# A token's own term in a chunked RWKV attention: from products by tokens in place of score columns with u

## The chip, the cores and the metric

The kernel runs on one core of a Trainium2 chip. The core's engines, which run side by side and meet at semaphores, are TensorE (PE, with its weight loads PEld), VectorE (DVE), ScalarE (ACT), GpSimd (POOL) and SyncE (SP, which here only starts DMAs). The metric is the device time in microseconds; lower is better. All numbers are float32.

## The reference, cut to what matters

The first half is an RWKV-5 recurrence over 768 tokens, for 4 batches and 8 heads of width 48; the second is a router that sends each of the 3072 tokens to one of 8 experts.

```python
for t in range(S):                                   # S = 768, B = 4, H = 8, D = 48
    kt, vt, rt = (k[:, :, t], v[:, :, t], r[:, :, t])
    cur = np.einsum('bhd,bhe->bhde', u[None] * kt, vt)
    y[:, :, t] = np.einsum('bhd,bhde->bhe', rt, state + cur)
    state = w[None, :, :, None] * state + np.einsum('bhd,bhe->bhde', kt, vt)
x = y.transpose(0, 2, 1, 3).reshape(B * S, H * D)    # 3072 x 384
# router: the expert with the largest cosine to x, gate = its softmax weight
# out[rows of e] = gate * (relu(x @ w1[e]) @ w2[e])
```

The term with `u` joins a token with itself alone: it adds `(sum over d of u[d] * k[t,d] * r[t,d]) * v[t]` to `y[t]`. That sum is one number for a token and a head. It is the part of the work that the change treats.

## The kernel before, in words

**Chunks and turns.** The 768 tokens are cut into 6 chunks of 128. A turn is one chunk for two of the four batches (`u` = 0 or 1 inside the turn, not to be confused with the input `u`), so there are 12 turns, 0 to 11. Turns of even number bring the first two batches of a chunk, odd ones the other two. In a chunk the decay is taken apart into a power of `w` that scales K and one that scales R (`kpow`, `rpow`, tables that are built once), so that the product of a scaled K and a scaled R carries the decay between the two tokens. A chunk is worked in two halves `s` of 64 tokens, and heads in pairs `p` with a parity `par`.

**One turn.** For turn t the work is: load K, R, V (SP); scale R and K by tokens on POOL (`scale_r` L376-379, `scale_k` L371-373: 128x384 each, two of each in a turn); turn them so that the width stands on the partitions (`turn_in` L390-393, transposes on PE into the PSUM banks `D`); take them out of PSUM (`take_in` L396-410, ACT copies, 128x512 each, into `RT` and `KT`); the scores (`scores` L425-440, PE); mask them to what lies before the token (`mask` L447-451, VectorE, four of 128x256); the outer products for the state (`outer` L460-472, PE), which VectorE adds (`half_state`, `next_state` L479-490) and POOL decays (`decay_state` L493-496); and a turn later the values times the scores (`with_v` L515-528), the state times R (`with_state` L531-545), the turning back (`turn_y` L554-558), and what the router needs (`take_x`, `keep_x`, `squares`, then in every second turn the logits and the choice of an expert in small VectorE steps).

**The own term.** `RT` holds two kinds of R side by side, index `j`: plain, and times `u*w`. The second is made by `own_r` (L413-422): a VectorE product of 128x512 that reads PSUM, two in a turn (in turn 0 eight ACT scalings instead). A score matmul therefore has 128 moving columns, 64 of each kind (L433-436), and writes both into one bank. `own_terms` (L454-458) then puts the diagonal of the second kind into the masked scores `AT`: four predicated copies of 128x256 in a turn, whose data lie in PSUM.

**Banks and order.** There are eight PSUM banks: four `D`, two `U`, two `Y`. `turn_in` writes the same `D` banks as the scores, so the transposes for turn t+1 wait until `mask` and `own_terms` of turn t have read them. The order on every engine is written out by hand: `plan.at(time, function)` gives each piece a place in a turn of `PERIOD = 9.4`, the pieces are sorted by that number and issued in that order. The numbers are places in a queue and not times; each engine then works through its queue as its waits allow. In a turn that begins with its scores at 0 and 0.9, the next turn's `turn_in` stand at 3.3, 3.77, 5.65 and 6.12, `with_v` at 1.8 and 4.25, `with_state` at 2.3, `outer` at 4.75 and `turn_y` of the turn before at 6.65 and 7.1. On POOL the next turn's scalings stand at 1.0, 2.0, 3.0 and 4.0 and the decay at 6.8; the first scaling also waits for the first scores of the running turn, by a dependency set by hand (L378-379).

**Around it.** Before the turns `build_first` (L82-132) loads `w` and `u` as columns in 4-byte pieces, builds the tables and the first loads; `tables_rows` turns them into `kpow` and `rpow`. After the turns come the experts, which keep PE busy until the outputs are scattered.

## Time and profile before

| | us |
|---|---|
| median of 3 runs | 421.48 |
| lowest and highest of them | 415.93, 426.96 |
| the profiled execution | 415.55 |
| its span | 413.7 |
| start of the scores of turn 0, of turn 11 | 8.81, 115.69 |
| TensorE clock granted, mean | 0.964 |

The start of a turn below is the start of its first score matmul in the timeline of PE: 8.81, 15.49, 24.25, 34.94, 44.41, 55.28, 64.70, 76.14, 85.28, 95.75, 105.70, 115.69 for turns 0 to 11. From turn 3 to turn 11 that is 80.75 us for four pairs of turns, 20.2 us a pair. Matmuls count as two records each in the trace, so that the 32 score matmuls of a turn are 64 records.

The rows of the groups of instructions that the change touches, cut from the view of groups with shapes kept apart; the columns are line, engine, operation, output <- inputs, shapes, count, then busy us and mean ns of one, then idle time before them:

```profile
L433 PE MATMUL ps<-RT,KT 48*64 48x128 f32 x768 | 25.3, 275 | 0.2
L448 DVE TENSOR_TENSOR AT<-ps,smask 128x256 f32<-128x256 f32 x48 | 18.6, 414 | 1.2 <-PE ps L433 1.2
L418 ACT ACTIVATE RT<-RT,uw 128x128 f32<-128x128 f32 x8 | 2.5, 390 | 0.0
```

### The profile page before, as it was taken

The page shows a single profiled execution, that of the slowest core. Times are in us where ns is not written, and L with a number is a line of the kernel's source. Part 1 is how long each engine was busy: PE and PEld are TensorE (multiplying, and loading weights), DVE is VectorE, ACT ScalarE, POOL GpSimd, SP SyncE. Part 2 cuts the span into 40 slices and gives each one's busy share as a digit, 9 for nine tenths or more (in the row PEclk, how much of TensorE's full clock was granted, in tenths as well). Part 3 has the DMA queues.
Part 4 walks back from the last instruction along what each step waited for, and adds up shares of the span by engine and source line. Part 5 has one row for each costly group of instructions (what it writes and reads, how often), then busy time and mean ns, then how long its engine had stood idle before and what let it go on. Part 6 is the DMA issues. An engine that isn't in the chain of part 4 may idle for free.

```text
span 413.7 us, 12753 instructions
## 1 busy us (share of the span) xinstructions
PE 383.0 (93%) x5055; PEld 349.9 (85%) x5055; DVE 236.4 (57%) x603; ACT 138.2 (33%) x357; POOL 189.2 (46%) x222
## 2 busy tenths in 40 slices
PE   8889899999989996999989997699999999999993
PEld 5778788888878895989779997699999989989982
DVE  7957787878885650532843744155546546465331
ACT  4464546465524521221023212221321321422410
POOL 3875656555530354420377427501753855702002
PEclk9999999999996996899999999689999999999998
DMA  9988788788154573263953553144454446101001
GB/s 157 198 165 174 158 172 181 146 183 179 44 178 142 162 238 104 73 164 93 315 178 90 126 182 93 42 111 136 132 137 142 144 133 199 62 10 57 0 2 65
DMA packets 100232, 54.44 MB, mean 132 GB/s; under 512 B 80897, under 2 KB 95275, under 8 KB 100162
## 3 DMA queue, kind: packets, MB, share of 16 engines
q1 hardware_dynamic: 93218, 43.68, 41.6%
q0 software_dynamic: 4448, 9.45, 7.5%
q8 instruction: 42, 0.69, 0.7%
q10 hardware_dynamic: 2496, 0.40, 0.5%
q14 instruction: 28, 0.23, 0.2%
HBM read 44.25 MB, written 9.58 MB: 130 GB/s over the span
## 4 chain that ended last, share of the span: by engine, by line
PE 76%; issue 9%; DVE 2%; another core or an unknown queue 2%; POOL 1%; ACT 1%; POOLq 0%; DVEq 0%; ACTq 0%
PE ps L1243 9%; PE ps L1383 8%; PE ps L1165 7%; PE ps L1364 6%; PE pu L1243 5%; PE ps L433 4%; PE ps L393 4%; PE pu L1383 4%; PE py L1243 4%; PE py L1383 3%; PE pu L558 3%; PE py L524 3%; PE py L1165 3%; PE py L543 2%; PE pu L469 2%
## 5 line engine op out<-in xcount | busy, mean ns | idle before, releaser
L1123 POOL DMA_INDIRECT G<-xs,quarters x76 | 83.7, 1101 | 50.5 <-issue 38.8
L1342 POOL DMA_INDIRECT out_dram<-y,goes x27 | 28.3, 1048 | 97.0 <-DVE y L1352 41.3
L1165 PE MATMUL ps<-RT,w 128*128 128x128 f32 x204 | 30.1, 299 | 4.4 <-ACT R L1168 1.9
L1165 PEld LDWEIGHTS ps<-RT,w 128*128 128x128 f32 x204 | 27.3, 210 | 5.9 <-issue 2.3
L377 POOL TENSOR_TENSOR Rw<-R,rpow 128x384 f32<-128x384 f32 x22 | 22.8, 1037 | 14.2 <-PE ps L433 8.0
L1243 PE MATMUL ps<-xTe,w 128*128 128x192 f32 (+3 forms) x132 | 27.0, 339 | 0.0
L433 PE MATMUL ps<-RT,KT 48*64 48x128 f32 x768 | 25.3, 275 | 0.2
L433 PEld LDWEIGHTS ps<-RT,KT 48*64 48x64 f32 x768 | 21.1, 132 | 3.7 <-issue 2.5
L373 POOL TENSOR_TENSOR Kw<-K,kpow 128x384 f32<-128x384 f32 x22 | 23.8, 1081 | 0.5 <-DMA R<-in_r_dram 0.5
L1243 PEld LDWEIGHTS ps<-xTe,w 128*128 128x128 f32 x132 | 23.4, 194 | 0.1
L496 POOL TENSOR_TENSOR T<-T,wC 128x384 f32<-128x384 f32 x10 | 8.3, 827 | 27.1 <-DVE T L490 27.1
L448 DVE TENSOR_TENSOR AT<-ps,smask 128x256 f32<-128x256 f32 x48 | 18.6, 414 | 1.2 <-PE ps L433 1.2
L409 ACT COPY RT<-ps 128x512 f32<-128x512 f32 x22 | 12.9, 585 | 18.3 <-PE ps L393 16.9
L455 DVE COPY_PREDICATED AT<-dmask,ps 128x256 f32<-128x256 int32 x48 | 18.5, 441 | 0.0
L1270 ACT ACTIVATE RT<-RT 128x384 f32<-128x384 f32 (+1 forms) x18 | 9.5, 532 | 26.1 <-DVE RT L1182 18.6
L1243 PE MATMUL ps<-Tx,S 128*128 128x192 f32 (+3 forms) x76 | 16.5, 348 | 1.2 <-issue 1.1
L420 DVE TENSOR_TENSOR RT<-ps,uw 128x512 f32<-128x512 f32 x22 | 15.2, 690 | 4.2 <-ACT RT L409 3.9
L393 PE MATMUL ps<-ident,Rw 128*128 128x128 f32 x96 | 15.4, 283 | 2.2 <-DVE AT L455 1.0
L1383 PE MATMUL ps<-T,RT 128*128 128x192 f32 x96 | 17.3, 327 | 0.0
L1270 ACT ACTIVATE hT<-hT 128x432 f32<-128x432 f32 (+2 forms) x18 | 9.7, 541 | 21.2 <-DVE hT L1182 16.1
L1383 PEld LDWEIGHTS ps<-T,RT 128*128 128x128 f32 x96 | 15.9, 190 | 0.9
L469 PE MATMUL pu<-V,Kw 64*64 64x48 f32 x704 | 14.4, 218 | 2.4 <-issue 2.3
(380 smaller groups left out, 917.0 us busy)
## 6 DMA issues: line engine op xcount, KB each, us to landing
w<-in_moe_w_dram SPq DMA_DIRECT2D x96, 128.0 KB
w<-in_moe_w_dram SPq DMA_DIRECT2D x24, 384.0 KB
xs<-X SPq DMA_DIRECT2D x24, 192.0 KB
K<-in_k_dram SPq DMA_DIRECT2D x32, 96.0 KB
R<-in_r_dram SPq DMA_DIRECT2D x32, 96.0 KB
V<-in_v_dram SPq DMA_DIRECT2D x32, 96.0 KB
w<-in_moe_w_dram SPq DMA_DIRECT2D x16, 192.0 KB
V<-in_v_dram SPq DMA_DIRECT2D x8, 192.0 KB
```

Source lines behind the costliest of these rows:

```text
L373: q.tensor_mul(of(k.Kw, t)[:, u, :, 0:D], of(k.K, t)[:, u] if t else raw(k, 0)[:, u, :, 0:D], k.kpow)
L377: ins = k.nc.gpsimd.tensor_mul(of(k.Rw, t)[:, u, :, 0:D], of(k.R, t)[:, u], k.rpow)
L393: k.last = k.nc.tensor.transpose(bank[:, p * C : (p + 1) * C], pair(src[:, u], p), k.ident)
L433: ins = k.nc.tensor.matmul(k.D[2 * u + par][halves(s), p * C : (p + 1) * C], KT[rows, u, p, halves(s)], RT[rows, u, p, s].rearrange("q j i ...
L469: k.last = k.nc.tensor.matmul(k.U[s][par * DP : (par + 1) * DP, col : col + D], Kw[halves(s), u, h, :], V[halves(s), u, h, 0:D], start=Tru ...
L1123: k.nc.gpsimd.indirect_dma_start(out=k.GG[e % 2][:, g * QUARTER : (g + 1) * QUARTER], out_offset=None, in_=k.xs.rearrange("n (q c) -> (n q ...
L1165: k.last = k.nc.tensor.matmul(ps, w1[:, m, f * 128 : (f + 1) * 128], x_of(k, e, m)[:, cols], start=(m == 0), stop=(m == NK - 1))
L1243: k.last = nc.tensor.matmul(ps[:, i * h : (i + 1) * h], a[:, g, i * 128 : (i + 1) * 128], b, start=start and i == 0, stop=True, skip_group ...
L1270: nc.scalar.activation(out(i, c), out(i, c), ACT.Relu)
L1342: k.nc.gpsimd.indirect_dma_start(out=out[:, :], out_offset=IndirectOffsetOnAxis(ap=k.goes[0:n, e, t : t + 1], axis=0), in_=y[0:n, :], in_o ...
L1364: k.last = k.nc.tensor.matmul(k.two[e][m], a, b, start=(f == 0), stop=(f == NF - 1))
L1383: k.last = nc.tensor.matmul(ps, a(q), b[:, q], start=start and q == 0, stop=True, skip_group_check=True,)
```

## The change

The own term no longer goes through the scores. Each token's K and R, as they lie by tokens, are multiplied (`product`: 128x384, on POOL, but for one of turn 0 on VectorE), then multiplied by `u` (turn 0, whose K and R are unscaled) or `u*w` (`with_u`, VectorE, in place), and summed over the 48 of a head (`own_sums`, VectorE, 128x384 to 128x8). `own_terms` now spreads these sums along the diagonal: one predicated copy of 128x512 for each `u`, with its data in SBUF, in place of two of 128x256 with their data in PSUM. `own_r` and the second kind in `RT` go; a score matmul has 64 moving columns. The room of the second kind holds the products `KR`. `u` comes as a row of 384 and is spread to all partitions by a matmul with a row of ones and an ACT copy (`spread_u`, twice); the row of `w` for it, loaded later before, is loaded at the start. `kp` is made by ACT as a reversed copy. The K scaling of turn 0 goes from VectorE to POOL.

The order of a turn changes: one `turn_y` of two moves behind the first scores of the next turn but one (with its `take_x`, `keep_x`, `squares`), the four `turn_in` are put between other pieces, `with_state` and `outer` are each cut in two, and `half_state` stands behind the second `outer`. `choose_a` of the chunk before the last moves from 1.0 to 2.3.

```diff
-        for dst, src in ((wc, k.w), (uw, k.u)):
-            for s in range(2):
-                q = nc.sync if s == 0 else nc.scalar
-                q.dma_start(out=dst[s * DP : s * DP + D, :], in_=src.rearrange("(p s) d -> s d p", s=2)[s])
+        for s in range(2):
+            q = nc.sync if s == 0 else nc.scalar
+            q.dma_start(out=wc[s * DP : s * DP + D, :], in_=k.w.rearrange("(p s) d -> s d p", s=2)[s])
+    k.w_row, k.u_row, k.uw_row = k.X[2][0:1, 1], k.X[2][0:1, 0], k.X[1][0:1, 1]
+    for q, dst, src in ((nc.sync, k.w_row, k.w), (nc.scalar, k.u_row, k.u)):
+        q.dma_start(out=dst, in_=src.rearrange("(o h) d -> o (h d)", o=1))
...
+    nc.gpsimd.tensor_scalar(k.uw_row, k.w_row, W_MIN, W_MAX, ALU.max, ALU.min)
+    nc.gpsimd.tensor_mul(k.uw_row, k.uw_row, k.u_row)
...
-    kp = scratch(k.YT[1], 1, NP)
-    nc.vector.tensor_mul(kp, t[:, :, ::-1], over_i)
     rp = scratch(k.YT[0], 0, NP)
     nc.vector.tensor_mul(rp, t, over_i)
-    k.uw = k.aconst.tile([128, NP], F32, name="uw2")
-    nc.vector.tensor_mul(k.uw, uw, wc)
+    kp = scratch(k.YT[1], 1, NP)
+    nc.scalar.copy(kp, rp[:, :, ::-1])
...
+def spread_u(k, i):
+    k.nc.tensor.matmul(k.Y[i][:, 0:DM], k.ones[0:1, :], (k.u_row, k.uw_row)[i], start=True, stop=True)
+    k.nc.scalar.copy(k.u_all[:, i], k.Y[i][:, 0:DM].rearrange("q (h d) -> q h d", h=H))
...
 def scale_k(k, t, u):
-    q = k.nc.gpsimd if t else k.nc.vector
-    q.tensor_mul(of(k.Kw, t)[:, u, :, 0:D], of(k.K, t)[:, u] if t else raw(k, 0)[:, u, :, 0:D], k.kpow)
+    k.nc.gpsimd.tensor_mul(of(k.Kw, t)[:, u, :, 0:D], of(k.K, t)[:, u] if t else raw(k, 0)[:, u, :, 0:D], k.kpow)
...
-def own_r(k, t, u):
-    if t == 0:
-        for p in range(NP):
-            R = of(k.RT, t)[:, u, p]
-            k.nc.scalar.mul(R[:, :, 1, :], R[:, :, 0, :], k.uw[:, p : p + 1])
-        return
-    k.nc.vector.tensor_mul(
-        of(k.RT, t)[:, u, :, :, 1, :], k.turned[u][0].rearrange("q (p s i) -> q p s i", p=NP, s=2),
-        k.uw[:, :, None, None].to_broadcast([128, NP, 2, HC]),
-    )
+def product(k, t, u):
+    a, b = (of(k.Kw, t), of(k.Rw, t)) if t else (raw(k, 0), raw(k, 1))
+    q = k.nc.vector if (t, u) == (0, 1) else k.nc.gpsimd
+    q.tensor_mul(of(k.KR, t)[:, u], a[:, u, :, 0:D], b[:, u, :, 0:D])
+def with_u(k, t, u):
+    q = k.nc.gpsimd if (t, u) == (0, 0) else k.nc.vector
+    KR = of(k.KR, t)[:, u]
+    q.tensor_mul(KR, KR, k.u_all[:, 1 if t else 0])
+def own_sums(k, t, u):
+    k.nc.vector.reduce_sum(of(k.own, t)[:, u], of(k.KR, t)[:, u], axis=AX.X)
...
-                    k.D[2 * u + par][halves(s), p * C : (p + 1) * C], KT[rows, u, p, halves(s)],
-                    RT[rows, u, p, s].rearrange("q j i -> q (j i)"),
+                    k.D[2 * u + par][halves(s), p * HC : (p + 1) * HC], KT[rows, u, p, halves(s)],
+                    RT[rows, u, p, s],
...
-def own_terms(k, t, u, par):
+def own_terms(k, t, u):
+    shape = [128, 2, NP, HC]
     k.nc.vector.copy_predicated(
-        of(k.AT, t)[:, u, par].rearrange("q (p i) -> q p i", p=NP),
-        k.dmask[:, None, :].to_broadcast([128, NP, HC]), kinds(k, u, par)[:, :, 1],
+        of(k.AT, t)[:, u].rearrange("q r (p i) -> q r p i", p=NP),
+        k.dmask[:, None, None, :].to_broadcast(shape),
+        of(k.own, t)[:, u].rearrange("q (p r) -> q r p", r=2)[:, :, :, None].to_broadcast(shape),
     )
...
-            plan.at(before + (4.0 if t else 4.75) + 2.6 * u, own_r, k, t, u)
+                if t:
+                    plan.at(before + ((2.75, 3.8), (5.3, 6.35))[u][place], turn_in, k, t, u, which)
+                    plan.at(before + ((3.4, 4.4), (6.1, 6.8))[u][place], take_in, k, t, u, which)
...
+            if t:
+                plan.at(before + 5.0 + u, product, k, t, u)
+                plan.at(before + 6.9 + 0.5 * u, with_u, k, t, u)
+                plan.at(before + 7.0 + 0.5 * u, own_sums, k, t, u)
+            else:
+                when = (before + 4.0, at + 2.3)[u]
+                for i, fn in enumerate((product, with_u, own_sums)):
+                    plan.at(at + 1.55 if (u, i) == (0, 2) else when + 0.01 * i, fn, k, t, u)
...
-                plan.at(at + 1.65 + 1.5 * u + 0.4 * par, own_terms, k, t, u, par)
+            plan.at(at + 1.65 + 1.5 * u, own_terms, k, t, u)
...
-            plan.at(at + 4.75, outer, k, t)
-            plan.at(at + 5.6, half_state, k, t)
+            for u in range(2):
+                plan.at(at + 4.75 + u, outer, k, t, (u,))
+            plan.at(at + 6.16, half_state, k, t)
...
-            plan.at(nxt + a[1], with_state, k, t)
+            for s in range(2):
+                plan.at(nxt + a[1] + s, with_state, k, t, (s,))
...
-                plan.at(nxt + a[5] + 0.45 * u, turn_y, k, t, u)
+                over = u * (P + 0.5 - a[5])
+                plan.at(nxt + a[5] + over, turn_y, k, t, u)
...
+    plan.at(-P + 3.2, spread_u, k, 0)
+    plan.at(1.0, spread_u, k, 1)
     for u in range(2):
-        plan.at(0.05 + 0.01 * u, scale_k, k, 0, u)
+        plan.at(0.05 + 2.0 * u, scale_k, k, 0, u)
```

## The prediction

> **What bounds the kernel now.** I read the page's busy shares first, then busy time in one stretch per turn, then the timeline of two turns.
>
> ```profile
> PE 383.0 (93%) x5055; PEld 349.9 (85%) x5055; DVE 236.4 (57%) x603; ACT 138.2 (33%) x357; POOL 189.2 (46%) x222
> ...
> 44.41:55.28 10.87, 9.79 (x317) 8.77 (x317) 7.32 (x21) 6.52 (x20) 6.57 (x9) 1.00 0.80 168
> 55.28:64.70 9.42, 9.42 (x293) 8.44 (x289) 8.07 (x22) 4.38 (x13) 5.14 (x5) 1.00 0.77 165
> 64.70:76.14 11.44, 10.05 (x317) 8.83 (x316) 8.08 (x27) 6.52 (x20) 6.93 (x10) 1.00 0.81 169
> 76.14:85.28 9.14, 9.14 (x297) 8.30 (x293) 8.08 (x22) 4.42 (x13) 5.19 (x5) 1.00 0.76 163
> ```
>
> The first line shows busy time by engine. The others give, per turn (4 to 7): length, then busy time of PE, PEld, VectorE, ACT and POOL with counts, the clock, the DMA share. In turns 5 and 7 TensorE is busy for the whole turn; in 4 and 6 it lacks 1.1 and 1.4 us, mostly "issue", in which nothing in the trace holds it. So in the turns TensorE is the bound, and its work is worth its own length. VectorE's busy 8 us leave about 2.
>
> ```profile
> 57.77 0.69 PE L524 MATMUL py<-AT,V 64*64 64x64 f32 x32
> 58.28 0.63 PE L543 MATMUL py<-RT,T 48*48 48x64 f32 x32
> 58.73 0.63 PE L543 MATMUL py<-RT,Tmid 48*48 48x64 f32 x32
> 61.72 1.10 PE L469 MATMUL pu<-V,Kw 64*64 64x48 f32 x64
> 64.70 2.28 PE L433 MATMUL ps<-RT,KT 48*64 48x128 f32 x64
> ```
>
> Timeline of PE: start, duration, what. The 64 score records of a turn take 1.9 to 2.3 us. The next lines stand 0.45 us apart for 32 records with 64 moving columns and the same 48 rows.
>
> ```profile
> 45.70 1.00 POOL L377 TENSOR_TENSOR Rw<-R,rpow 128x384 f32<-128x384 f32 x1
> 45.86 0.88 DVE L665 TENSOR_TENSOR l<-l,inv 128x32 f32<-128x32 f32 x1
> 56.52 1.24 POOL L377 TENSOR_TENSOR Rw<-R,rpow 128x384 f32<-128x384 f32 x1 [1.29 <-PE ps L433]
> 56.82 1.49 DVE L844 TENSOR_TENSOR P<-slot,lo 128x512 f32<-128x512 f32 x1
> 57.72 1.47 POOL L373 TENSOR_TENSOR Kw<-K,kpow 128x384 f32<-128x384 f32 x1
> ...
> L665 DVE TENSOR_TENSOR l<-l,inv x6: 191/880/882, 45.9 to 141.0; 128x32 f32<-128x32 f32 x6
> L844 DVE TENSOR_TENSOR P<-slot,lo x6: 684/1086/1494, 56.8 to 141.1; 128x512 f32<-128x512 f32 x6
> L373 DVE TENSOR_TENSOR Kw<-Kw,kpow x2: 546/904/1262, 9.5 to 10.7; 128x384 f32<-128x384 f32 x2
> ```
>
> This is the second view that matters (durations in the last three lines: least, median, most, in ns). A VectorE step whose two inputs both lie in SBUF takes 191 ns alone and 880 beside a POOL product; it ends as that product ends (45.86 + 0.88 = 46.74 against 46.70). `P` costs 684 alone and 1494 between two scalings, and the POOL product behind it 1.47 in place of 1.0. They take turns.
>
> **What the skill says.** The Trainium skill, SBUF — State Buffer, section "Who interferes with whom": a VectorE instruction with two SBUF inputs contends with a GpSimd one that reads SBUF; the second waits for the first to end; with one SBUF input it does not; a reduction never does. The trace agrees on the first: 880 against 191. It also agrees that masks, with one input in PSUM, are free: 407 to 425 ns beside any POOL work. VectorE: DVE Perf Modes, section "The TRN2 errata — SBUF-src ops pay a fixed extra latency per instruction", has (N+151)/0.96 ns for an fp32 two-input product: 557 for 384, 691 for 512. The trace has 546 and 684. TensorE: Matmul & The Clock Gate, "Part 3: Packing small matmuls — row/col tiling": matmuls in different parts of the array run together. The trace agrees: 64 records of 269 ns pass in 1.91.
>
> **The change part by part.**
>
> *TensorE.* Scores at 64 columns: 64 records x 0.45/32 = 0.90 for 1.91, so -1.0 us a turn, -12 over 12 turns; all of it is on the path while TensorE is the bound. `spread_u` adds 2 x 2 records at 384 columns; 12 such took 3.87 (chain, line 1364), so 0.65 each. The first stands ahead of turn 0's transposes and lies open: +0.65. The new order has the same matmuls; I cost it at nothing, since transposes and small matmuls never waited for each other in turns 5 and 7.
>
> *VectorE.* Gone in a turn: two `own_r`, 0.60 apart in the timeline, and four copies, 0.33 apart: 2.5. Added: two copies of 512, not in the trace. Lower bound 0.60 (as `own_r`, same size), upper 0.69 (formula): 0.60, plus 0.07 each since they follow the second mask at once: 1.34. Two `with_u` at 0.55 (row L373 alone), two sums. The nearest reduction, of 384, took 0.528; I take 0.53. A step that needs the one before stood 0.66 behind it (`half_state`, `next_state`), an independent one 0.46: 2 x (0.66 + 0.46) = 2.24. Net +1.1 a turn. Over a pair of turns VectorE's queue was full for 16.9 us (20.86 between turns 5 and 7, less 3.97 of listed idle), 1.2 of it waits for POOL. So 15.7 + 2.2 = 17.9 of own work, beside TensorE's 20.2 - 2.0 = 18.2.
>
> *POOL.* +2 products a turn of the kind of `scale_k` and `scale_r`, 1.0 each (0.965 from start to start): busy 5.9 to 7.9 a turn. In turn 0: product, `with_u` and two scalings, 4.0, ahead of or between the scalings for turn 1. Two one-row steps for `uw_row` not in the trace, between 0.2 (small memset) and 1.0 (product of the same 384): 0.6 each, hidden by waiting for K and R.
>
> *The shared port.* A ledger per pair of turns. POOL's reads: before 8 x 0.965 + 2 x 0.83 = 9.4, now 12 x 0.965 + 1.66 = 13.2. (The `pow` of `choose_a` is not counted: at 116.5 `P` took its 0.69 beside it.) VectorE's steps with two SBUF inputs: before `P` 0.60, `QV` 0.34 and nine small ones at 0.2, 2.7; now also 4 x 0.6 of `own_terms`, whose data move from PSUM to SBUF, and 4 x 0.5 of `with_u`: 7.1. Sum 12.1 before, 20.3 now, against 20.2 a pair today. That is the core of it. `own_terms` stands at 1.65 and 3.15, amid POOL's scalings at 1.0 to 4.0, `with_u` beside the second product and the decay. No trace shows a predicated copy waiting for POOL: the bounds are nothing (then 17.9 in the ledger) and one POOL product, 0.97, each. I take half a product. With eight new steps that is 3.9 if POOL is always at work; POOL reads 13.2 of 20.2, so 2.5. VectorE: 17.9 + 1.2 + 2.5 = 21.6 if none hides in present idle; about 0.7 hides in waits for PE that shorten, so 20.9. What queues behind a waiting `own_terms` is the next two masks; turn_in of the next turn waits for them, and then the scores. So I take 20.9 a pair, +0.7, over the five pairs of turns 1 to 10: +3.5.
>
> *Start.* ACT's eight scalings (8.36 to 10.90) no longer hold scores 0, and VectorE's masks no longer stand behind two K scalings (9.50 to 11.23): -1.5, bound -2.5. But POOL must do 9 products in turn 0, from 8.5 on, then four memsets of V (1.05) and two more products; its first scaling for turn 2 starts at about 19.5, not 16.73, and scores 2 follow it: +2.8. With 0.65 for `spread_u`, +2. DMA: 768 pieces of 4 bytes less 384, two rows of 1.5 KB moved ahead of K and R on SP's and ACT's queues (issue 0.26 each): nothing either way, within 0.5, since K and R are met first by matmuls that end at 6.07.
>
> *End.* Turn 11 has no scalings beside it: its scores keep their -1.0. `turn_y`, its squares and `choose_a` move by up to 1.3 places, still before `choose` at 4.2. ACT's moved steps (copies 0.48, squares 0.52) lie in its idle time: it is busy 4.4 to 7 of 10 us. Weight loads hang on PE's progress and move along. Experts: unchanged. -1.
>
> *Sum:* +3.5 + 2 - 1 = +4.5 on the profiled 415.55: 420. The median of the runs shown, 421.48, is 1.4% above that execution, so a median of **426**.
>
> **Rivals.** *A, the saving stays (faster).* The waits for POOL fall into time that VectorE would idle, or the copies don't hold the port. Then TensorE sets 18.2 + 0.3 a pair: -1.7 x 5.5 = -9.4, -1 at the end, +1 at the start: -9.5, median 412. For it: TensorE's bound is plain. Against it: the ledger, and VectorE's 17.9 leaves only 0.3 for waits. *B, POOL and the port become the chain (slower beyond 2%).* Each VectorE step with two inputs, the small ones of the router too, meets a POOL product and they alternate. In the 19 steps of a pair with half a product each at 80% that is 7.4 of waits, less the 2.5 + 1.2 counted: +3.7, of which half shifts into idle: 22.7 a pair, +2.5 x 5 = +12.5, with +2 - 1: +13.5, median 435. It decides from +1.5 a pair on, 21.7. For it: `P` and `l` already meet a product nearly each time (medians 1086 and 880). Against: POOL stops after its six products until the decay. *C, the scores don't get shorter,* since the weight loads (133 ns for 64 columns, 120 in lines 543) set their pace: 64 loads of 120 pass in 0.90, so 64 of 133 in about 1.0, and 0.9 is saved all the same; small, and inside the ranges of the others.
>
> **How the numbers follow.** The likeliest case, a near balance a little slower, 0.50: 420 to 432. A 0.22: 407 to 417. B 0.28: 429 to 445. The range 411 to 438 leaves about 0.1 below (the lower half of A) and 0.1 above (the upper third of B). Two percent, 8.4 us, is about what a measurement of this kernel can tell from no change: its three runs spread by 2.6%. Faster: the larger part of A and none else, 0.18. Slower: most of B and a tenth of the middle case, 0.31. Within: 0.51.
>
> **What would show it.** In the changed profile: 64 score records in about 0.9 to 1.1 us (else C). `own_terms` at 0.6 to 0.7 alone and up to 1.7 with POOL at work; if all 24 stay under 0.75, the copy doesn't hold the port, and A gains. `with_u` between 0.55 and 1.5. VectorE full in the turns and TensorE no longer: waits of PE's transposes for AT, KT or POOL's Kw of over 0.3 a turn. Pairs of turns at 20.9; 18.5 shows A, over 21.7 B. First scaling for turn 2 at 19 to 20. Wrong would be: turns of 9.2 with PE still full.

## The result, and the profile after

The changed kernel takes 456.86 us median (452.92 to 460.29, 5 runs); beside it the kernel before took 420.1 (412.85 to 426.96, 5 runs). The ratio is 1.095, with a 95% interval from 1.081 to 1.109: slower. The median lies above the predicted range (426, 411 to 438). (Executions of one kernel fall into a faster and a slower state, and a ratio with an interval is taken over the faster ones alone, so that it is not the quotient of the medians.) The profiled execution of the changed kernel has a span of 455.0 us, 41.3 more than the 413.7 of before. Line numbers below are those of the changed kernel (`scores` L448, `turn_in` L403, `mask` L459, `with_u` L434, `own_sums` L438, `own_terms` L468, `product` L428).

Busy time by engine, from the page, to set beside the line of before:

```profile
PE 398.9 (88%) x5059; PEld 355.9 (78%) x5059; DVE 264.3 (58%) x600; ACT 140.9 (31%) x352; POOL 228.3 (50%) x250
```

TensorE's share falls from 93% to 88%, although its records are as many as before but for four more (the two matmuls of `spread_u`), and those of the scores are narrower. Where the time lies is seen from the starts of the turns. Scores 0 start 1.2 us later than before (9.97), scores 2 5.2 later (29.47), scores 11 40.8 later (156.46). From scores 11 to the end it is 298.5 us, before 298.0. So 35.6 of the 41.3 us lie in turns 2 to 10, which go from 91.4 to 127.0 us. (One more profile of each kernel, on another chip, splits its 42.4 us into 4.8 up to scores 2, 32.5 in turns 2 to 10 and 5.2 after them.) Busy time in one stretch per turn, for turns 4 to 7 (columns as in the prediction: length, busy PE, PEld, VectorE, ACT, POOL, clock, DMA):

```profile
57.42:68.62 11.20, 9.83 (x318) 8.05 (x317) 9.98 (x25) 6.68 (x18) 10.73 (x12) 1.00 0.71 151
68.62:85.53 16.91, 13.16 (x294) 11.10 (x290) 10.45 (x25) 4.97 (x13) 7.26 (x9) 0.70 0.41 91
85.53:96.67 11.14, 9.97 (x317) 8.23 (x317) 9.92 (x25) 6.66 (x18) 10.71 (x12) 1.00 0.70 152
96.67:112.61 15.94, 12.26 (x293) 10.20 (x289) 10.33 (x25) 4.96 (x13) 6.55 (x7) 0.79 0.46 97
```

Even turns are little longer than the 10.87 and 11.44 of before; turns 5 and 7 take 16.91 and 15.94 where they took 9.42 and 9.14. VectorE is busy 10.45 and 9.92 us in turns 5 and 6, 20.4 for the pair, about what was foretold. But the pair takes 28.05 us: none of the engines is busy for all of a long turn, and the clock granted to TensorE is 0.70 and 0.79 in them. Turns 2, 9 and 10 are long too (17.8, 16.9 and 16.2). The timeline of turn 5 shows how, TensorE first, then VectorE, then GpSimd (start, duration, what, and in brackets the idle time before it and what ended it):

```profile
72.11 0.63 PE L557 MATMUL py<-RT,T 48*48 48x64 f32 x32
75.50 1.08 PE L403 MATMUL ps<-ident,Rw 128*128 128x128 f32 x4 [2.76 <-DVE AT L459]
76.38 1.81 PE L881 MATMUL pu<-QV,P 128*128 128x64 f32 x8
78.11 1.11 PE L557 MATMUL py<-RT,Tmid 48*48 48x64 f32 x32
79.15 1.11 PE L403 MATMUL ps<-ident,Kw 128*128 128x128 f32 x4
...
84.16 0.66 PE L403 MATMUL ps<-ident,Kw 128*128 128x128 f32 x4
```

```profile
68.57 0.59 DVE L434 TENSOR_TENSOR RT<-RT,u_all 128x384 f32<-128x384 f32 x1
...
69.49 0.98 DVE L848 SCALAR_TENSOR_TENSOR lo<-hi,rank 128x4 f32<-128x4 f32 x1
...
70.48 0.54 DVE L438 TENSOR_REDUCE own<-RT 128x8 f32<-128x384 f32 x1
...
72.46 1.15 DVE L872 TENSOR_TENSOR QV<-HV,cum_oh 128x256 f32<-128x256 f32 x1
73.54 1.48 DVE L858 TENSOR_TENSOR P<-slot,lo 128x512 f32<-128x512 f32 x1
74.94 0.74 DVE L459 TENSOR_TENSOR AT<-ps,smask 128x256 f32<-128x256 f32 x2
```

```profile
69.45 1.00 POOL L387 TENSOR_TENSOR Rw<-R,rpow 128x384 f32<-128x384 f32 x1
70.42 1.00 POOL L383 TENSOR_TENSOR Kw<-K,kpow 128x384 f32<-128x384 f32 x1
71.38 1.00 POOL L387 TENSOR_TENSOR Rw<-R,rpow 128x384 f32<-128x384 f32 x1
72.34 0.99 POOL L383 TENSOR_TENSOR Kw<-K,kpow 128x384 f32<-128x384 f32 x1
73.30 2.58 POOL L428 TENSOR_TENSOR RT<-Kw,Rw 128x384 f32<-128x384 f32 x2
```

Read from below: GpSimd now runs six products without a break. Above it VectorE works without a break from 68.57, pushed back by the own-term steps; `lo` (128x4) takes 0.98 and ends with a product; `P` takes 1.48, where it takes 0.68 alone, and a product ends within it, at 74.47. The masks, whose scores had been done since about 70.5, start at 74.94. TensorE's transposes wait for them, 2.76 us. What comes after that wait is the second loss: a group of four transposes takes 1.08 to 1.11 rather than 0.66, and 32 small matmuls pass in 1.04 (79.15 less 78.11) rather than the 0.59 of turn 4 (63.38 less 62.79), until 84.16. The clock doesn't fall at the end of the wait: in turn 5 the granted clock drops during it, at 73.89, in turn 7 at 104.61, 1.06 us after it. Such a row of slow records, 4.9 to 8.7 us long, follows the long wait in each of the five long turns (6.65 in turn 2, 2.76 in 5, 7 and 9, 3.11 for a router step in 10).

The start shows the same on a smaller scale. In turn 0 the transposes for turn 1 wait 2.12 us for a mask, which stands behind three own-term steps on VectorE (`product`, `with_u` and `own_sums`, 13.19 to 15.79):

```profile
16.28 1.09 PE L403 MATMUL ps<-ident,Rw 128*128 128x128 f32 x4 [2.12 <-DVE AT L459]
```

From there to 26.10, well into turn 1, the granted clock is 0.50.

Over turns 2 to 10, who waited for whom (us in total, times, longest):

```profile
PE ps L403 <- DVE AT L459: 15.7, 6, 6.7
```

```profile
DVE Tmid L499 <- PE pu L483: 27.0, 9, 5.8
```

TensorE waits for VectorE, and then VectorE waits for TensorE.

### The profile page after: what moved, and what is told of

Same layout as the page of the kernel before. It is cut to its first block, busy times and chain, and to the rows that moved or that the text cites. A ratio compares the mean times of both kernels' runs of the same rounds, so it can differ in the third digit from the quotient of the medians.

```text
span 455.0 us, 12789 instructions
## 1 busy us (share of the span) xinstructions
PE 398.9 (88%) x5059; PEld 355.9 (78%) x5059; DVE 264.3 (58%) x600; ACT 140.9 (31%) x352; POOL 228.3 (50%) x250
## 4 chain that ended last, share of the span: by engine, by line
PE 66%; DVE 14%; issue 12%; POOL 2%; ACT 2%; SPq 1%; DMA 1%; POOLq 0%; another core or an unknown queue 0%; DVEq 0%; ACTq 0%
PE ps L1275 9%; PE ps L1415 7%; PE ps L403 6%; PE ps L1197 6%; PE ps L1396 6%; PE pu L1275 4%; PE pu L1415 4%; PE pu L483 3%; PE py L1275 3%; PE py L1415 3%; PE py L538 3%; PE py L557 3%; DVE RT L434 2%; PE py L1197 2%; DVE own L438 2%
## 5 line engine op out<-in xcount | busy, mean ns | idle before, releaser
L403 PE MATMUL ps<-ident,Rw 128*128 128x128 f32 x96 | 19.5, 338 | 18.2 <-DVE AT L459 18.2
L403 PEld LDWEIGHTS ps<-ident,Rw 128*128 128x128 f32 x96 | 12.8, 169 | 20.6 <-POOL RT L428 15.4
L428 POOL TENSOR_TENSOR RT<-Kw,Rw 128x384 f32<-128x384 f32 x23 | 27.8, 1226 | 0.0
L459 DVE TENSOR_TENSOR AT<-ps,smask 128x256 f32<-128x256 f32 x48 | 24.0, 650 | 0.0
L468 DVE COPY_PREDICATED AT<-dmask,own 128x512 f32<-128x512 int32 x24 | 21.9, 912 | 0.9
L499 DVE TENSOR_TENSOR Tmid<-T,pu 128x384 f32<-128x384 f32 x10 | 5.5, 552 | 27.0 <-PE pu L483 27.0
L1275 PEld LDWEIGHTS ps<-Tx,S 128*128 128x128 f32 x76 | 13.5, 197 | 7.4 <-ACT kept L1293 5.3
L483 PE MATMUL pu<-V,Kw 64*64 64x48 f32 x704 | 19.1, 250 | 0.0
L403 PE MATMUL ps<-ident,Kw 128*128 128x128 f32 x96 | 18.9, 329 | 0.0
L483 PEld LDWEIGHTS pu<-V,Kw 64*64 64x64 f32 x704 | 16.7, 165 | 2.7 <-issue 2.5
L538 PE MATMUL py<-AT,V 64*64 64x64 f32 x704 | 18.5, 255 | 0.0
```

The source lines that it names most:

```text
L403: k.last = k.nc.tensor.transpose(bank[:, p * C : (p + 1) * C], pair(src[:, u], p), k.ident)
L428: q.tensor_mul(of(k.KR, t)[:, u], a[:, u, :, 0:D], b[:, u, :, 0:D])
L459: k.nc.vector.tensor_mul(of(k.AT, t)[:, u, par].rearrange("q (p i) -> q p i", p=NP), k.D[2 * u + par][:, 0 : NP * HC].rearrange("q (p i) - ...
L483: k.last = k.nc.tensor.matmul(k.U[s][par * DP : (par + 1) * DP, col : col + D], Kw[halves(s), u, h, :], V[halves(s), u, h, 0:D], start=Tru ...
L538: k.last = k.nc.tensor.matmul(y_out(k, t, par, p, u, s), V[halves(s), u, 2 * p + par, :], AT[halves(s), u, par, p * HC : (p + 1) * HC], st ...
L1275: k.last = nc.tensor.matmul(ps[:, i * h : (i + 1) * h], a[:, g, i * 128 : (i + 1) * 128], b, start=start and i == 0, stop=True, skip_group ...
```

## The experiments

Two theories came from this. **P**: the own-term steps make VectorE late (by their own length and at the port that it shares with GpSimd), TensorE stands, and standing costs its clock. **O**: the new order costs TensorE time by itself. A third thing was seen in turn 2, where one small VectorE step took 6.44 us. Times are set beside runs of the kernel before on the same chip at about the same time. Those of `e1` to `e6`, `e14` and `e15` are of one execution each, those of `e7` to `e13` medians of four. "Turns" is the time from scores 2 to scores 11 in one profile: 91.4 before and 127.0 after in the profiles above. Repeats of both kernels on another chip gave 94.5 and 126.9, so that some 3 us of it are noise.

### Order and change apart

`e1_old_order` is the changed kernel with the order of before:

```diff
-plan.at(before + ((2.75, 3.8), (5.3, 6.35))[u][place], turn_in, k, t, u, which)
+plan.at(before + 3.3 + 2.35 * u + 0.47 * place, turn_in, k, t, u, which)
...
-    plan.at(at + 4.75 + u, outer, k, t, (u,))
+plan.at(at + 4.75, outer, k, t)
...
```

> The changed kernel with the order of a turn put back as it was before (own terms still from products). Theory P, VectorE held up by GpSimd at the shared port, so that TensorE waits 2.8 us in turns 2, 5, 7, 9 and 10 and its clock then falls: the late masks are still there, the long turns stay at 15 to 17 us, total 445 to 458. Theory O, the new order makes TensorE itself slower by cutting tiled matmuls between full-array transposes: each turn loses 1 to 1.5 us, 12 to 15 in all, and some gaps close, total 425 to 440.

`e2_order_alone` is the kernel before with the order of the change:

> The kernel before with the new order of a turn alone (own terms still from the scores with u). P: no product, no wait at the port: within 5 us of the kernel before. O: the 32-record pieces of a turn stand 0.55 to 0.6 us apart in place of 0.45, some 14 pieces a turn, so turns are longer by 1 to 1.5 us and the total by 10 to 16.

Measured, beside 396.77 for the kernel before: 420.13 with the old order, 399.31 for the order alone; turns 114.6 and 98.5. So the order alone costs the turns 4 to 7 us, and of the whole less than single executions can tell; the change without its order costs 23. (The totals expected of e1 and, below, of e3 were higher; here the kernel before, too, was 23 us faster than in the result.) With the order back, the transposes wait for a mask in turn 2 alone (7.3 us). In the changed order groups of small matmuls alternate with full transposes. In turn 4 of e2 a group of four transposes takes 0.55 to 0.59 us, in turn 5 of the kernel before 0.43 to 0.53; 32 records of the outer products pass in 0.56 to 0.61 rather than 0.52. That the rest of what the order does to the changed kernel comes through longer waits is my reading; no run isolates it.

### The clock

`e3_kept_warm` puts 12 useless matmuls into the wait of turns 5, 7 and 9 of the changed kernel:

```diff
+def busy(k):
+    for _ in range(12):
+        k.nc.tensor.matmul(k.U[0][:, 0:128], k.ident, k.ones, start=True, stop=True, skip_group_check=True)
...
+            if u and t in (5, 7, 9):
+                plan.at(at + 2.31, busy, k)
```

> The changed kernel with 12 matmuls of no use (128x128, into a free bank) in turns 5, 7 and 9, issued just ahead of the transpose that waits for the masks. If the clock that falls after the gap is what makes these turns long: their clock stays at 1.00, the wait stays, and they go from 16.9, 15.9 and 16.9 us to 12.3 to 13.3 each, total 443 to 446. If the clock is no cause (the pieces after the gap are slow for another reason): the turns stay at 16 to 17 and the total at 455 to 458.

It took 424.86 beside 396.77, turns 119.3. TensorE in turn 5, where the useless matmuls (L460) fill the wait, and then the three turns, in stretches as above:

```profile
76.28 2.94 PE L460 MATMUL pu<-ones,ident 128*128 128x128 f32 x24
79.12 0.63 PE L403 MATMUL ps<-ident,Rw 128*128 128x128 f32 x4
```

```profile
72.23:85.34 13.11, 12.12 (x318) 10.56 (x314) 10.35 (x25) 4.89 (x13) 7.27 (x9) 1.00 0.56 120
97.69:110.80 13.11, 12.35 (x317) 10.68 (x313) 10.35 (x25) 4.89 (x13) 6.57 (x7) 1.00 0.54 116
122.18:135.30 13.12, 12.45 (x318) 10.74 (x314) 10.37 (x25) 4.90 (x13) 6.57 (x7) 1.00 0.29 69
```

With more work TensorE is done sooner: 13.11, 13.11, 13.12 for 16.91, 15.94, 16.88, the clock at 1.00, VectorE's busy time as it was. The masks come as late as before (the transposes start 6.89 us after the scores, as against 6.88); what is gone, 2.8 to 3.8 us a turn, is the price of the clock. The two turns between them became 1.2 and 0.6 longer, so that over turns 5 to 8 a pair falls from 27.4 to 25.0 us. That price varies by itself: in the repeat of the changed kernel turn 7 had a wait of 2.67 us, a clock of 0.87 and a length of 13.63.

Which waits cost the clock can be read from all 19 profiles together, between scores 0 and scores 11. After every wait of TensorE of 2.3 us or more the granted clock was halved, at the latest 1.7 us after its end. After shorter ones it was halved in some cases (1.32 us in e4, 1.67 in e14) and not in others (2.04 in e6, 2.26 in e8).

### The own-term steps left out, together and apart

`e4_no_products` leaves `product`, `with_u` and `own_sums` out of the changed kernel:

> The changed kernel with product, with_u and own_sums left out (the sums are zero, so the own term is missing from the output); the copies, the narrow scores and the new order stay. P: GpSimd reads four times a turn as before, VectorE has 2.2 us a turn less: no gap over 1 us on TensorE, clock 1.00 in the turns, turns of 9.3 to 10.2 us, total 408 to 418. O: the turns stay at 10.5 to 11 us from the order alone, total 422 to 432.

Turns: 100.8 of 127.0. (The total, 709.77, follows from the tokens' other experts and isn't comparable; nor are those of the next two.) The 26.2 us between are the three steps' doing. What is left, 11.2 us a turn, is more than either theory had: the transposes still wait 5.0 us for masks, and turns 5 and 7 still lose some clock (0.86, 0.87). Two more runs split the 26.2. `e14_no_sums` leaves out `with_u` and `own_sums`, so that the sums stay at zero, and GpSimd's products stay:

```diff
-plan.at(before + 6.9 + 0.5 * u, with_u, k, t, u)
-plan.at(before + 7.0 + 0.5 * u, own_sums, k, t, u)
```

> The changed kernel, in the order of the change, with the products with u and the sums left out (four VectorE steps a turn, 2.2 us alone); GpSimd's products and the predicated copies stay. The own terms are then zero, the router sends tokens elsewhere and the experts' part can't be compared; only the turns are read. If VectorE's length is what costs: turns 2 to 10 at 102 to 109 us, near the 100.8 of the run without products, with u and sums, and where the changed kernel takes 127. If GpSimd's two more products and its share of the port cost most: 117 or more.

`e15_no_products` leaves out GpSimd's products, and VectorE's steps stay:

```diff
-plan.at(before + 5.0 + u, product, k, t, u)
...
-    q.tensor_mul(KR, KR, k.u_all[:, 1 if t else 0])
+    q.tensor_mul(KR, of(k.Kw, t)[:, u, :, 0:D] if t else KR, k.u_all[:, 1 if t else 0])
```

> The changed kernel, in the order of the change, with GpSimd's products left out from turn 1 on; the steps with u take the scaled K in their place, so that VectorE keeps all its steps and GpSimd its four scalings a turn. The own terms are wrong, and only the turns are read. If VectorE's length is what costs: turns 2 to 10 at 116 to 124 us (less than 127, since fewer VectorE steps meet a product of GpSimd). If GpSimd's two more products and the port cost most: 108 or less.

Turns: 107.0 without VectorE's four steps, 119.7 without GpSimd's two. Turns 4 and 5 of each, the run without VectorE's steps first:

```profile
52.11:63.49 11.38, 9.86 (x317) 8.05 (x317) 8.39 (x21) 6.83 (x19) 10.24 (x13) 1.00 0.72 150
63.49:74.68 11.19, 9.63 (x294) 7.98 (x290) 8.28 (x18) 4.90 (x13) 8.03 (x8) 1.00 0.64 137
```

```profile
54.52:65.72 11.20, 9.84 (x318) 8.06 (x317) 9.99 (x25) 6.79 (x19) 8.35 (x10) 1.00 0.73 152
65.72:80.92 15.20, 12.24 (x294) 10.41 (x290) 9.64 (x25) 4.96 (x13) 4.72 (x7) 0.78 0.47 102
```

In the first pair GpSimd is as busy as in the changed kernel (10.24, 8.03), VectorE 1.6 to 2.2 us less, and turn 5 keeps its clock; its 11.19 us are about those of the order alone (11.32 in e2). (Turn 7 of this run still loses clock, 0.76, after a wait of 1.67 us, and takes 14.19.) In the second GpSimd is relieved by 2.4 and 2.5 us, VectorE only in turn 5, by 0.8, and turn 5 stays long. Both lie in the ranges set for the case that VectorE's length is what costs. VectorE's steps carry 20.0 of the 26.2 us, GpSimd's products 7.3 (the two overlap by about 1).

### The port

`e8_sums_in_psum` writes the sums to PSUM, so that the predicated copies have one input in SBUF; `e9_products_vectore` makes the products on VectorE. Both stand on `e7_memsets_later` below, which has the old order.

```diff
-    k.nc.vector.reduce_sum(of(k.own, t)[:, u], of(k.KR, t)[:, u], axis=AX.X)
+    k.nc.vector.reduce_sum(k.D[2 * u][:, 256 : 256 + H], of(k.KR, t)[:, u], axis=AX.X)
...
-        of(k.own, t)[:, u].rearrange("q (p r) -> q r p", r=2)[:, :, :, None].to_broadcast(shape),
+        k.D[2 * u][:, 256 : 256 + H].rearrange("q (p r) -> q r p", r=2)[:, :, :, None].to_broadcast(shape),
```

> As the run with the memsets moved, and the sums of the own terms are written to PSUM (columns 256 to 263 of the bank of the scores), so that the predicated copies have one input in SBUF rather than two. If the predicated copies' waits for POOL's products at the shared port are a main part of the loss: none of the 24 above 0.85 us (they reached 1.41), and turns 2 to 10 together 4 us or more shorter than in the run with the memsets moved. Rival (the loss is VectorE's queue as a whole, the products with u and the router's steps, and the copies carry little of it): within 2 us of that run. The transposes now wait for the copies too, which can cost up to 0.7 us a turn, 6 in all, in either case.

```diff
-    q = k.nc.vector if (t, u) == (0, 1) else k.nc.gpsimd
+    q = k.nc.vector if t or u else k.nc.gpsimd
```

> As the run with the memsets moved, but VectorE makes all products of K and R, none but the first is POOL's. POOL then has its four scalings a turn as before, VectorE two more steps of 0.55 us alone. If POOL's unbroken run of six products and its share of the port is what costs: the gain on the VectorE steps beside it outweighs the 1.1 us a turn, turns 2 to 10 are 2 us or more shorter than in the run with the memsets moved. Rival (VectorE's own length is what costs): 20.1 us of own work a pair of turns, more waits of the transposes for masks, turns 2 to 10 longer by 4 to 10 us.

Beside 416.49 for the kernel before they took 447.63 (ratio 1.075, interval 1.060 to 1.090) and 443.55 (1.062, 1.051 to 1.074); e7 took 443.6, but its four executions lie between 432.69 and 447.45, so that the three totals can't be told apart. Turns: 116.2 and 108.9, e7 110.6. The port itself behaves as the Trainium skill has it (SBUF — State Buffer, "Who interferes with whom"). These two rows give the copies' least, median and most ns with the data in SBUF (the changed kernel) and in PSUM (e8):

```profile
L468 DVE COPY_PREDICATED AT<-dmask,own x24: 731/758/1411, 12.1 to 161.5; 128x512 f32<-128x512 int32 x24
```

```profile
L468 DVE COPY_PREDICATED AT<-dmask,ps x24: 728/737/764, 12.4 to 151.8; 128x512 f32<-128x512 int32 x24
```

With two inputs in SBUF the copy can wait for a product, with one it doesn't. But that is little: seven of the 24 copies of the changed kernel took 1.12 us or more, the others 0.73 to 0.82, and the mean is 0.91 us as against 0.74 in e8, some 4 us over the whole run. e8 didn't gain them. Its scores now wait 3.2 us for the sums in the same banks, and its clock falls more often (0.83 over turns 3 to 10, 0.91 in e7); the transposes wait for the copies only 0.3 us, far less than the 6 that I had allowed for. e9 fits neither theory: VectorE was busy for 96.7 us of the turns rather than 90.4, GpSimd for 58.4 rather than 82.2, and the turns came out 1.7 us shorter, which one profile of each can't tell from nothing.

### Turn 2: a step that was held

In turn 2 of the changed kernel a VectorE step of 128x24, which took 0.17 us before, lasts 6.44 us, until GpSimd's six products are over, and the masks stand behind it. `e5_casts_later` moves it behind `next_state`, past the masks; `e6_old_order_casts` does so with the old order:

```diff
-    plan.at(P + 8.7, cast_consts, k)
+    plan.at(2 * P + 6.25, cast_consts, k)
```

> The changed kernel with cast_consts moved from the head of turn 2, where its last step took 6.44 us in front of the masks, to behind next_state of turn 2, where GpSimd waits. If that step was held by GpSimd's unbroken run of products: it takes about 0.2 us, turn 2 falls from 17.8 to 10 to 11, total 6 to 8 us below the changed kernel. If it was slow by itself it takes 6 us again.

> The changed kernel with the old order of a turn and cast_consts moved. If order, the held step and the clock add up: about 14 us below the changed kernel for the order (as 420 against some 433 in the first group) and 6 to 8 for the step, so 12 to 18 us above the kernel before remain for the products and the port.

They took 456.24 and 435.95, where the repeats of after and before took 456.86 and 414.51. The hoped-for 6 to 8 us did not come: turn 2 took 18.2. (e6, 20.3 us below e5 and 14.2 in the turns, shows the share of the order once more.) The hold had moved on to the next step (VectorE and GpSimd of e5):

```profile
31.49 6.54 DVE L468 COPY_PREDICATED AT<-dmask,own 128x512 f32<-128x512 int32 x1
```

```profile
31.50 0.19 POOL L285 MEMSET ent<- 128x128 f32 x1
31.67 0.98 POOL L387 TENSOR_TENSOR Rw<-R,rpow 128x384 f32<-128x384 f32 x1
32.62 0.99 POOL L383 TENSOR_TENSOR Kw<-K,kpow 128x384 f32<-128x384 f32 x1
```

But TensorE's wait behind this hold was short, and the longer one was for GpSimd's first scaling:

```profile
32.71 1.11 PE L403 MATMUL ps<-ident,Rw 128*128 128x128 f32 x4 [2.94 <-POOL Rw L387]
...
38.48 1.08 PE L403 MATMUL ps<-ident,Rw 128*128 128x128 f32 x4 [0.69 <-DVE AT L459]
```

From 32.71 to the end of the turn the granted clock was 0.50. So in e5 a late GpSimd and the lost clock made turn 2 as long as the hold had.

Both held steps had come up as GpSimd ran a memset ahead of the products, or was about to. `e7_memsets_later`, with the old order and the casts moved, takes the memsets from there:

```diff
-    plan.at(P + 6.9, embeddings_a, k)
+    plan.at(2 * P + 6.1, embeddings_a, k)
...
-    plan.at(2 * P + 6.0, embeddings_b, k)
+    plan.at(2 * P + 6.2, embeddings_b, k)
```

> The changed kernel with the old order, the casts moved as before, and the two memsets of the embeddings (lines 283 and 285, which stand just ahead of POOL's six products of turn 2) put behind these six products. Theory (a VectorE step that begins to wait while POOL runs a memset just ahead of a run of products is held through the whole run): no VectorE step of turn 2 above 1.6 us, turn 2 at 10 to 12 us where it was 17.4, the ratio to the kernel before at 1.02 to 1.03 where it was 1.04. Rival (any step that begins in an unbroken run of six products can be held through it, and the memset has no part in it): again a step of over 4 us in turn 2, turn 2 at 17 to 18, ratio 1.04.

No VectorE step of turn 2 exceeds 1.47 us now, as the theory had it; turn 2 still takes 17.4, and the quotient of the medians is 1.065, where 1.02 to 1.03 was expected. TensorE waits 2.1 us for masks, since VectorE's `with_u` ahead of them waits for a product that GpSimd, full in turns 1 and 2, brings late, and 4.3 us for the embeddings that the experiment itself put behind the products. So the hold was real, but taking it away did not shorten turn 2. How long the turn would be with neither the hold nor the wait that replaced it isn't shown.

The other profiles narrow the theory. In turn 2 of all 13 profiles of the changed kernel and its variants that keep the two memsets ahead of the products, one VectorE step is held, for 3.73 to 6.57 us, until the last product; in the three without them (e7, e8, e9) none is. But in four of the 13 the step came up only when the memsets were over (in e12 0.45 us after them). And in turn 5 of the changed kernel two other memsets (L67) stand directly ahead of six products, and `lo` was held by one product alone. So memsets ahead of the products go with the hold, but they are not enough for it, and the step need not come up during them.

### Is it the place in VectorE's queue, or its length?

The masks stood behind own-term and router steps, so moving them forward should have freed TensorE. `e10_masks_first_old` and `e11_masks_first_new` put all four masks of a turn first, and the own-term steps and the choice of an expert behind:

```diff
-    plan.at(at + 0.9 + 1.5 * u + 0.36 * par, mask, k, t, u, par)
+    plan.at(at + 0.9 + 0.02 * u + 0.01 * par, mask, k, t, u, par)
...
+    plan.at(then + 1.0, choose, k, c)
+    plan.at(then + 4.3, ranks, k, c)
```

> The changed kernel with the old order and the casts later; in VectorE's queue the four masks of a turn now stand first, and the products with u, the sums, the predicated copies, the choice of an expert and the steps HV, QV and P behind them (the matmul with P moves to 4.6, that of the ranks to 4.3). No step is removed. Theory (TensorE stands still because the masks, which its transposes wait for, queue behind VectorE's own-term and router steps, and its clock falls after these gaps): waits of the transposes for masks under 2 us in turns 2 to 10 together, turns 2 to 10 together at most 102 us where the same without it took 110.7, ratio to the kernel before at most 1.03 where it was 1.04 to 1.06. Rival (VectorE's length is the bound, and the order of its queue only says which wait shows it): the waits move to P, to the state or to the scores, turns 2 to 10 stay at 108 to 113 us, ratio 1.04 to 1.07.

> The same with the order of the change kept: only VectorE's queue has the masks first. Theory: the wait of the transposes for masks goes from 15.7 us in turns 2 to 10 to under 3, no odd turn takes above 13 us (they took 16 to 17), turns 2 to 10 together at most 108 us where they took 127, ratio at most 1.05 where it was 1.095. Rival (VectorE's length): turns 2 to 10 at 118 us or more, ratio 1.075 or more.

They took 467.84 and 473.87 beside 410.04 (ratios 1.147, 1.134 to 1.159, and 1.150, 1.135 to 1.165), turns 138.9 and 144.1. The first is worse than either theory had it; the second lies in the rival's open range (118 or more), but for another reason. No wait of the transposes for masks is left, but TensorE waits for copies of ScalarE (10.8 and 15.3 us), which stand behind an exponential that itself waits for VectorE's choice of an expert, and for VectorE's reads of the U banks. I had moved more than the suspect. `e12_own_late_old` and `e13_own_late_new` move the own-term steps alone:

```diff
-    plan.at(before + 6.9 + 0.5 * u, with_u, k, t, u)
-    plan.at(before + 7.0 + 0.5 * u, own_sums, k, t, u)
+    late = at + 4.0 + 0.1 * u if t < TURNS - 1 else before + 6.9 + 0.5 * u
+    plan.at(late, with_u, k, t, u)
+    plan.at(late + 0.01, own_sums, k, t, u)
...
-            plan.at(at + 1.65 + 1.5 * u, own_terms, k, t, u)
+            plan.at(at + 4.02 + 0.1 * u if 0 < t < TURNS - 1 else at + 1.65 + 1.5 * u, own_terms, k, t, u)
```

> The changed kernel with the old order and the casts later; only the own-term steps of VectorE (products with u, sums, predicated copies of turns 1 to 10) move: from places ahead of and between the masks to 4.0 of the turn, behind the last mask and behind the router's reads of the U banks. The choice of an expert, HV, QV and P keep their places; nothing is removed. VectorE's queue ahead of the masks is then what it is in the kernel before. Theory (the own-term steps, put ahead of and between the masks, make the masks late, and with them TensorE's transposes): waits of the transposes for masks under 3 us in turns 2 to 10 together, turns 2 to 10 at most 103 us where they took 110.7, ratio to the kernel before at most 1.03. Rival (VectorE's length bounds the turns wherever these steps stand): 108 us or more, ratio 1.04 or more, the waits at P, at the state or at the state's decay.

> The same with the order of the change kept: only the own-term steps on VectorE move behind the masks. Theory: the long turns 5, 7 and 9 fall from 16 to 17 us to 13 or less, turns 2 to 10 to at most 113 us from 127, ratio at most 1.065 where it was 1.095. Rival (VectorE's length): 120 us or more, ratio 1.08 or more. If the old order is then faster than this by 8 us or more again, the order costs that much by itself beside these VectorE steps.

They took 443.18 and 450.66 beside 413.56, turns 114.8 and 120.5, where the same without the move took 110.7 (e6) and 125.0 (e5). In the old order my theory of the place falls and the rival of the length stands. In the order of the change a part of the theory came true: turns 5, 7 and 9 fell to 12.68, 12.85 and 11.64. But turns 4, 6 and 8 rose to 12.66, 13.93 and 12.28, and the whole stayed above the 113 that was asked for. Between the two orders 5.7 us are left, about what the order costs the kernel before. TensorE's waits in e12, and its turns 7 and 8:

```profile
PE pu L572 <- DVE Tmid L499: 14.6, 7, 4.1
...
PE ps L403 <- DVE AT L459: 0.3, 1, 0.3
```

```profile
94.95:106.67 11.72, 8.81 (x294) 7.72 (x290) 11.11 (x23) 4.62 (x12) 7.33 (x7) 1.00 0.63 131
106.67:118.60 11.93, 9.31 (x318) 7.81 (x317) 10.41 (x25) 6.64 (x19) 9.23 (x10) 1.00 0.70 143
```

The wait for the masks is gone, and 14.6 us of waiting for the state's sum stand in its place. VectorE is busy for 11.11 of 11.72 and 10.41 of 11.93 us: with the clock at 1.00 throughout, the pair still takes 23.65.

No version of the change came level with the kernel before; the nearest, e6 with the old order and the casts moved, took 435.95 beside 418.70 and 414.51, 4 to 5% more.

## Why the prediction was wrong, step by step

- **Scores.** 32 records of a half pass in about 0.6 us in the new order, 1.2 a turn, and 64 in 1.0 in the old one, where 0.9 was foretold. The saving is there, 0.7 of 1.0 us.
- **The pieces of VectorE and GpSimd** came as costed: the copy 0.73 alone and up to 1.41 (0.6 to 0.7 and 1.7 foretold), `with_u` 0.55 to 1.21, a sum 0.53 to 0.55. VectorE's pair at 20.4 us busy lies within the 21.6 of its reckoned queue.
- **The step that failed** is the one from there to the pair: "VectorE: 17.9 + 1.2 + 2.5 = 21.6 if none hides in present idle; about 0.7 hides in waits for PE that shorten, so 20.9." It took the length of the fuller queue for the length of the pair. With two engines nearly full and each feeding the other, the waits of one come on top of the work of the other: 15.7 us of TensorE for masks, then 27.0 of VectorE for TensorE. With the clock kept at 1.00 (e3, turns 5 to 8) a pair takes 25.0 us, though VectorE is busy for 20.1 of them and TensorE, without the useless matmuls, for about 19.4; in e12 (turns 7 and 8) it is 23.65. So of the 7.2 us by which a pair of turns 5 to 8 grew (20.2 to 27.4), 4.8 are there at full clock, and 2.4 come with the lost clock. VectorE's two `with_u` and two sums a turn, which this step priced into 0.7 us a pair, cost 20.0 us in turns 2 to 10 (e14).
- **What no step held** is the clock. A wait of TensorE was priced by its length; a wait of 2.76 us cost 2.8 to 3.8 more (e3).
- **"The new order has the same matmuls; I cost it at nothing"** failed too: 4 to 7 us in the turns (e2), and more in the changed kernel, whose turns are 12.4 shorter with the old order (e1).
- **Start:** +2 foretold, +5.2 at scores 2. The mechanism was right only in part. GpSimd's queue is as late as foretold and more: the first scaling for turn 2 stands at 21.02, foretold at 19 to 20, and ends at 22.33. But the mask that the same transposes wait for ends 0.07 us later still, and from 16.28 to 26.10 TensorE has half its clock after the wait for another mask, behind own-term steps of turn 0. "VectorE's masks no longer stand behind two K scalings", counted as a gain, left out that they now stand behind these steps. **End:** -1 foretold, +0.5 measured (+5.2 in the repeat), so that it can't be judged.
- **Rivals.** B ended on the right side and by the right engines, but at 22.7 a pair. What made 28 of it, TensorE standing long enough to lose its clock, was in no rival.

In sum: +5.2, +35.6 and +0.5 make the 41.3 us. Of the 35.6, the own-term steps carry 26.2 (e4) and the order up to 7.1 (e2); 2.3 are left for the rest, less than the runs can tell. Taken the other way round, the order first (e1), it is 12.4 for the order and 23.2 for the change without it: the two work through the same waits, and no single split is the right one.

Left open: why the order costs the changed kernel more than the kernel before, beyond the longer waits; and what holds a VectorE step through several products, beyond the memsets ahead of them.

## What to carry to other kernels

When a change makes a second engine nearly as full as the bound, and the two feed each other in every round, don't take the larger load for the round: add the waits in which each stands for the other, or test with the steps left out. Price a wait of TensorE together with the slow stretch that may follow it: in these runs 2.3 us was enough each time, and up to 3.8 us came on top. And when a wait ends at a step that is late, look at how busy that engine is before reordering it: here the full queue mostly showed the same lateness at another consumer.

## What the runs showed of the hardware that was not expected

- A wait of 2.76 us was enough to bring TensorE to half its clock for 6.0 to 8.7 us of work (32 records in 1.04 rather than 0.59 us). The Trainium skill (TensorE: Matmul & The Clock Gate, "Part 1: The HAM clock gate (the "warmup" mystery)") has half the clock after an idle window of about 3.4 us, and full clock again after about 3.4 us of sustained work. The kind agrees; here the wait was shorter and the slow stretch, with TensorE at work, longer.
- In turn 2 a VectorE step was held through six products of GpSimd that follow two memsets, 6.44 and 6.54 us, where the skill's section on interference lets the second of two instructions wait for the first. The first of these steps reads one tensor from SBUF only. The prediction gave the section's rule for one such input (no contention) without its exception, VectorE's two-port modes; no run shows in which mode this step ran.
